# Four output-weight loads of a segment wait for the fourth step of their product instead of the first

## The chip, the cores and the metric

The program runs on one core of a Trainium2 chip. Inside a core TensorE (PE in the profile) multiplies, with its weight loads shown as PEld; VectorE (DVE), ScalarE (ACT) and GpSimd (POOL) work on rows; SyncE (SP) only issues transfers. Sixteen DMA engines carry every transfer between HBM and the on-chip memory, whoever issues it. The metric is the device time of one execution in microseconds, as a median over runs.

## The reference

Four layers run one after the other on 2048 rows of 640 values, in the order A, B, A, B, each added to its own input. Layer A is attention with a memory that is carried from segment to segment; it is the layer that the change is in.

```python
mem = mem0                                   # 8 rows of 640
for s in range(n_seg):                       # 64 segments of 32 rows
    h = concat([mem, x[32*s:32*s+32]])       # 40 rows
    q, k, v = h @ Wq, h @ Wk, h @ Wv         # 32 heads of 192: three weights of 640 x 6144
    p = softmax(mask(q k^T * 192**-0.5))     # per head, 40 x 40
    o = (p v, all heads side by side) @ Wo   # 6144 x 640
    mem = o[:8]                              # enters the next segment
    outs.append(o[8:])
```

So the 64 segments of a layer A can't run side by side: the eight memory rows of one segment are the input of the next. Layer B is a linear attention without such a chain, and the change doesn't touch it.

## The kernel before

**Layers and stages.** Each layer A has a preparation (`A_pre`), which multiplies the last eight rows of every segment for all segments at once, and the chain (`A_chain`), which runs the 64 segments in turn. In the profile the two chains lie at about 210 to 1345 us and 1840 to 2985 us.

**One segment.** The 32 heads are worked in four rounds of eight heads, numbered by their place n = 0 to 3 in the segment. Even segments take the rounds in the order 0, 1, 2, 3 and odd ones in the order 3, 2, 1, 0, so that the last round's weights of one segment are the first round's of the next. For each place n PE makes three products, Q, K and V (`project`, the matmuls of L1092). A product has five steps, i = 0 to 4, one for each block of 128 of the 640 inputs, and a step is four matmuls on four strips of the array. Between them come the scores (`scores`, L1129), the weighting of the values (`attend`, L1142, and `attend_tails`, L1155) and the output product (`wo_round`, L1198), which adds each round's part to the bank `ps_w`. The order of all instructions is the one written (a manual schedule), engine by engine.

**Which weights stay and which are loaded.** Most of the weights lie on the chip for the whole chain. Rounds 0 and 3 share places: three blocks of Q, two of K and two of V (`SLOTS`), of 384 KB each, and blocks 4 to 11 of the output weight, which lie in `wo_both` and are loaded in four pieces of 320 KB. Every segment therefore loads seven blocks through `load_slot` (L725) and four pieces through `load_piece` (L774) from HBM, all issued by SP, in one order: Q, Q, Q, K, K, V, V and then the four pieces. The pieces come in the order that `load_both` gives, columns 1280, 2560, 3840 and then 0. Here they are called pieces 1 to 4.

**What releases a load.** A load may overwrite its place only when the first round has used it. Beyond that, each load waits for one chosen matmul, so that few are under way at once: the load is put on the list `held`, and `release` takes the first of the list and makes SP wait for the matmul it is given. The table `PACE` says, for a product (m, n), after which of its five steps the next held load is released:

```python
if PACE.get((m, n)) == i:
    self.release(last)          # last: the fourth matmul of step i
```

The seven blocks are released during Q0 to Q2 (that is, Q at place 0 to Q at place 2). `load_both` puts the four pieces on the list after the output product of the first round's blocks 4 to 11, which is the last reader of `wo_both`; they are then released one by one in the products K2, V2, Q3 and K3. In the last segment of each chain all its twelve remaining loads are released together by that output product, and the table does nothing to them.

**Who uses the pieces.** The output product of the last round comes at the end of the segment, as 24 matmuls of L1198 that read `QK`. It takes blocks 6 to 11 first (pieces 1 to 3), then blocks 0 to 5, so that piece 4 (blocks 4 and 5) is used by the last four matmuls. Blocks 0 to 3 are on the chip.

**Other transfers of a segment.** POOL issues small ones on a queue of its own: `Vp<-vb` (L1073), which brings the prepared value rows of the memory's tail, `kqb<-kqb` (L1062), the rows of the next segment and the stores of the results. PE's own instructions also arrive by DMA, as packets of the instruction queue.

Of the kernel before, what the change touches and what calls it, by code (L numbers as in the profile page):

```python
# [25 lines left out]

VH = 194

PACE = {("Q", 0): 0, ("K", 0): 1, ("V", 0): 3, ("Q", 1): 4, ("K", 1): 4, ("V", 1): 3, ("Q", 2): 1, ("K", 2): 0, ("V", 2): 0,
        ("Q", 3): 0, ("K", 3): 0}  # L30

STEPS = (2, 5)

# [92 lines left out]
class Kernel:  # L126
# [876 lines left out]
    def A_chain(self, xn_dram, at_dram, li, load_slot, piece, late_wo, load_both, wo, low):  # L1003
# [3 lines left out]
        with tc.tile_pool(name=f"A{li}_ch", reuse_waits="tile", bufs=1) as sp, \  # L1007
# [67 lines left out]
            def project(hT, ps, m, n, s, steps):  # L1075
# [3 lines left out]
                for i in steps:  # L1079
# [14 lines left out]
                    if n == 0 and b >= KC - ns:  # L1094
                        self.held.append(lambda b=b: load_slot(m, order[NR - 1], b))
                    if PACE.get((m, n)) == i:
                        self.release(last)
# [371 lines left out]
```

## Time and profile before

| | us |
|---|---|
| time, median of 3 runs | 3256.92 (3249.77 to 3258.15) |
| profiled execution, first to last instruction (its span; the profile gives no other time for it) | 3253.7 |
| PE busy in it | 3095.3 (95%) |
| PEld busy | 1980.2 (61%) |
| DVE busy | 2208.8 (68%) |
| ACT busy | 1883.0 (58%) |
| POOL busy | 1410.7 (43%) |
| mean load on the 16 DMA engines in the first chain (200 to 1340 us) | share 0.74, 247 GB/s |

The page of the profile gives busy times, the span in slices, the DMA queues, the chain of work that ended last and the costliest groups. Of a group the columns are line, engine, operation, out<-in, count, busy time, mean of one in ns, and the idle time of the engine before it with what ended most of it. In the timeline each row has its start and length in us, and in square brackets the idle time of the engine before it with what ended it; "issue" there means that nothing which the profile shows ended it. The view of one line or tile gives, for transfers, the least, median and greatest time from issue to landing.

### The profile page before, as it was taken

The page shows a single profiled execution, that of the slowest core. Times are in us where ns is not written, and L with a number is a line of the kernel's source. Part 1 is how long each engine was busy: PE and PEld are TensorE (multiplying, and loading weights), DVE is VectorE, ACT ScalarE, POOL GpSimd, SP SyncE. Part 2 cuts the span into 40 slices and gives each one's busy share as a digit, 9 for nine tenths or more (in the row PEclk, how much of TensorE's full clock was granted, in tenths as well). Part 3 has the DMA queues.
Part 4 walks back from the last instruction along what each step waited for, and adds up shares of the span by engine and source line. Part 5 has one row for each costly group of instructions (what it writes and reads, how often), then busy time and mean ns, then how long its engine had stood idle before and what let it go on. Part 6 is the DMA issues. An engine that isn't in the chain of part 4 may idle for free.

```text
span 3253.7 us, 140890 instructions
## 1 busy us (share of the span) xinstructions
PE 3095.3 (95%) x59424; PEld 1980.2 (61%) x59730; DVE 2208.8 (68%) x5457; ACT 1883.0 (58%) x4481; POOL 1410.7 (43%) x2920
## 2 busy tenths in 40 slices
PE   9989999999999999999999899999999999999999
PEld 7756666666666666555367566666666666665553
DVE  5557777777777777666643577777777777776465
ACT  3346666666666666646433466666666666666453
POOL 3345555555455455430122355555555554554300
PEclk9999999999999999999999999999999999999999
DMA  8977777777777777840385677777777777778400
GB/s 306 372 271 253 256 248 257 232 255 253 236 256 245 244 257 238 285 166 1 113 319 193 240 233 257 248 252 256 242 264 240 259 244 245 255 236 282 149 1 33
DMA packets 325018, 747.58 MB, mean 230 GB/s; under 512 B 65818, under 2 KB 100274, under 8 KB 321314
## 3 DMA queue, kind: packets, MB, share of 16 engines
q1 hardware_dynamic: 254850, 638.55, 56.1%
q0 software_dynamic: 67616, 86.77, 9.7%
q10 hardware_dynamic: 1920, 13.24, 1.0%
q8 instruction: 469, 7.68, 1.0%
q14 instruction: 163, 1.34, 0.1%
HBM read 668.80 MB, written 77.03 MB: 229 GB/s over the span
## 4 chain that ended last, share of the span: by engine, by line
PE 75%; DMA 11%; DVE 8%; issue 3%; ACT 3%; POOL 0%; SPq 0%; PEld 0%; DVEq 0%; POOLq 0%; ACTq 0%
PE ps_qk_q L1092 12%; PE ps_qk_k L1092 12%; PE ps_v L1092 11%; PE ps_w L1198 10%; DMA arena<-in_A_Wv_dram 6%; PE ps_pre L960 6%; PE ps_s L1129 5%; PE ps_o L1142 3%; PE ps_pre L989 3%; PE kv L1424 2%; DVE raws L1371 2%; PE ps_wo L444 2%; DMA Vp<-vb 2%; DMA arena<-wo_rows 2%; DVE hT L1373 2%
## 5 line engine op out<-in xcount | busy, mean ns | idle before, releaser
L1092 PEld LDWEIGHTS <-hT 128*32 128x32 bf16 x30720 | 792.6, 97 | 422.7 <-issue 43.0
L1112 DVE STREAM_TRANSPOSE QK<-raws 128x512 bf16<-128x512 bf16 (+1 forms) x1152 | 730.7, 643 | 207.3 <-ACT raws L1107 166.7
L1092 PE MATMUL ps_qk_q<-arena,hT 128*32 128x384 bf16 x10240 | 510.4, 327 | 38.2 <-DVE hT L1373 31.1
L1069 POOL COPY QK<-kqb 64x192 bf16<-64x192 bf16 x1024 | 350.4, 342 | 380.9 <-PE ps_s L1129 344.3
L1092 PE MATMUL ps_qk_k<-arena,hT 128*32 128x384 bf16 x10240 | 511.7, 328 | 3.1 <-issue 1.2
L1107 ACT ACTIVATE raws<-ps_qk_k 128x512 bf16<-128x512 f32 (+1 forms) x640 | 313.5, 510 | 253.1 <-PE ps_qk_k L1092 253.1
L1092 PE MATMUL ps_v<-arena,hT 128*32 128x384 bf16 x8192 | 435.2, 326 | 15.2 <-DMA arena<-in_A_Wv_dram 7.2
L1073 POOL DMA_DIRECT2D Vp<-vb x512 | 257.6, 503 | 416.3 <-PE ps_t L1155 252.0
L1172 ACT ACTIVATE raws<-ps_o,rc 128x192 bf16<-128x192 f32 x1024 | 373.4, 420 | 109.3 <-DVE rc L1166 104.8
L1107 ACT ACTIVATE raws<-ps_qk_q 128x512 bf16<-128x512 f32 x512 | 305.7, 597 | 164.5 <-PE ps_qk_q L1092 153.4
L1198 PE MATMUL ps_w<-arena,under 128*32 128x320 bf16 x6144 | 307.4, 300 | 16.7 <-issue 13.1
L1062 POOL DMA_DIRECT2D kqb<-kqb x512 | 290.6, 568 | 70.2 <-POOL QK L1069 50.2
L1121 DVE CAST Vp<-ps_v 64x384 bf16<-64x384 f32 x512 | 286.4, 559 | 37.9 <-ACT Vp L1119 22.8
L1129 PEld LDWEIGHTS <-QK 128*80 128x80 bf16 x4096 | 195.8, 121 | 161.4 <-issue 157.3
L1119 ACT ACTIVATE Vp<-ps_v 64x384 bf16<-64x384 f32 x512 | 246.4, 481 | 55.5 <-PE ps_v L1092 54.2
L1129 PE MATMUL ps_s<-QK 128*80 128x80 bf16 x4096 | 256.8, 210 | 5.4 <-POOL QK L1069 2.8
L1218 ACT ACTIVATE E<-ps_s 80x320 bf16<-80x320 f32 x512 | 217.6, 425 | 32.3 <-PE ps_t L1155 28.9
L1051 ACT ACTIVATE wh<-ps_w 64x160 f32<-64x160 f32 x256 | 76.6, 299 | 264.8 <-DVE raws L1371 254.9
L1058 POOL DMA_DIRECT2D attn<-under x128 | 91.6, 716 | 292.8 <-DVE under L1054 289.7
L960 PEld LDWEIGHTS <-arena 128*128 128x128 bf16 x1920 | 188.4, 98 | 32.4 <-DVE next_xT L97 4.6
L97 DVE CAST arena<-ps_pre 128x512 bf16<-128x512 f32 (+1 forms) x160 | 102.2, 646 | 143.5 <-PE ps_pre L960 96.4
L1142 PE MATMUL ps_o<-Vp,E 80*32 80x193 bf16 x4096 | 180.3, 248 | 13.2 <-DMA Vp<-vb 3.7
(159 smaller groups left out, 4586.2 us busy)
## 6 DMA issues: line engine op xcount, KB each, us to landing
arena<-wo_rows SPq DMA_DIRECT2D x560, 320.0 KB, 5.6
arena<-in_A_Wq_dram SPq DMA_DIRECT2D x427, 384.0 KB, 4.3
arena<-in_A_Wk_dram SPq DMA_DIRECT2D x298, 384.0 KB, 4.8
arena<-in_A_Wv_dram SPq DMA_DIRECT2D x290, 384.0 KB, 6.0
kqb<-kqb POOLq DMA_DIRECT2D x512, 48.0 KB, 4.9
vb<-arena POOLq DMA_DIRECT2D x128, 97.0 KB, 6.1
Vp<-vb POOLq DMA_DIRECT2D x512, 24.2 KB, 4.0
kqb<-arena SPq DMA_DIRECT2D x8, 1536.0 KB, 10.0
```

Source lines behind the costliest of these rows:

```text
L960: nc.tensor.matmul(ps[:, T * i:T * i + T], lhsT=w[b][:, P * c:P * c + P], rhs=xBT[:, b, :], start=(b == 0), stop=(b == KC - 1))
L1062: nc.gpsimd.dma_start(out=kqb[:], in_=self.kqb_d[r, :, s, :])
L1069: nc.gpsimd.tensor_copy(out=o, in_=kqb[h, :].rearrange("p (x c q) -> p x c q", c=3, q=16))
L1073: nc.gpsimd.dma_start(out=Vs[n % 2][64:80, :], in_=self.vb_d[s, r].rearrange("g t f -> (g t) f"))
L1092: last = nc.tensor.matmul(o, lhsT=hT[:, b, :], rhs=rhs, start=(i == 0), stop=(i == KC - 1), tile_position=(0, 32 * g), skip_group_check=True)
L1107: nc.scalar.activation(out=raw[:, c], in_=ps[:, c], func=ACT.Copy)
L1112: nc.vector.transpose(out=o, in_=i)
L1121: nc.vector.tensor_copy(out=o, in_=i)
L1129: nc.tensor.matmul(S[0:80, c0:c0 + 80], lhsT=KT[:, 4 * x + c, :], rhs=QT[:, 4 * x + c, :], start=(c % 2 == 0), stop=(c % 2 == 1), skip_gro ...
L1142: nc.tensor.matmul(O[G][32 * h:32 * h + 32, VH * G:VH * G + 193], lhsT=E[0:80, 80 * h + 32 * G:80 * h + 32 * G + 32], rhs=V[0:80, VH * h:V ...
L1172: nc.scalar.activation(out=out, in_=i, func=ACT.Copy, scale=rc[G])
L1198: step = nc.tensor.matmul(W[q:q + 32, 0:320], lhsT=OT[i // 6][:, i % 6 // 2, 32 * (i % 2):32 * (i % 2) + 32], rhs=rhs, start=(first and i ...
```

## The change

Four numbers of the table change: the four pieces of the output weight are released by step i = 3 of the products K2, V2, Q3 and K3, not by step i = 0. The same loads, in the same order on SP, wait for a matmul that stands twelve matmuls later in the same product. No instruction is added, removed or moved on any engine.

```diff
 PACE = {("Q", 0): 0, ("K", 0): 1, ("V", 0): 3, ("Q", 1): 4, ("K", 1): 4, ("V", 1): 3,
-        ("Q", 2): 1, ("K", 2): 0, ("V", 2): 0,
-        ("Q", 3): 0, ("K", 3): 0}
+        ("Q", 2): 1, ("K", 2): 3, ("V", 2): 3,
+        ("Q", 3): 3, ("K", 3): 3}
```

More of the change, by code (lines that the diff above doesn't have):

```diff
@@ L27 @@
 VH = 194
-PACE = {("Q", 0): 0, ("K", 0): 1, ("V", 0): 3, ("Q", 1): 4, ("K", 1): 4, ("V", 1): 3, ("Q", 2): 1, ("K", 2): 0, ("V", 2): 0,
-        ("Q", 3): 0, ("K", 3): 0}
+PACE = {("Q", 0): 0, ("K", 0): 1, ("V", 0): 3, ("Q", 1): 4, ("K", 1): 4, ("V", 1): 3, ("Q", 2): 1, ("K", 2): 3, ("V", 2): 3,
+        ("Q", 3): 3, ("K", 3): 3}
 STEPS = (2, 5)
```

## The prediction

> **What bounds the kernel now.** First the page: who is busy, and what the chain that ended last is made of.
>
> ```profile
> span 3253.7 us, 140890 instructions
> PE 3095.3 (95%) x59424; PEld 1980.2 (61%) x59730; DVE 2208.8 (68%) x5457; ACT 1883.0 (58%) x4481; POOL 1410.7 (43%) x2920
> ...
> q8 instruction: 469, 7.68, 1.0%
> ...
> PE 75%; DMA 11%; DVE 8%; issue 3%; ACT 3%; POOL 0%; SPq 0%; PEld 0%; DVEq 0%; POOLq 0%; ACTq 0%
> ```
>
> PE carries the span; the rest that can be had is 11% DMA and 3% "issue". So the second view is PE's list of waits (total us, times, longest us).
>
> ```profile
> PE ps_w L1198 <- issue: 25.1, 40, 1.6
> PE ps_w L1198 <- DMA arena<-wo_rows: 9.4, 17, 1.2
> ...
> PE ps_v L1092 <- DMA arena<-in_A_Wv_dram: 7.2, 18, 0.9
> PE ps_v L1092 <- issue: 7.0, 12, 1.2
> ...
> PE ps_o L1142 <- DMA Vp<-vb: 3.7, 10, 1.0
> ...
> PE ps_o L1142 <- issue: 3.0, 3, 1.1
> ```
>
> The waits that a weight load can touch are few: 7.2 us for V blocks, 9.4 us for output weights (some of them in the chains' last segments, which the table doesn't reach), 3.7 us for the small `Vp` loads, and 35.1 us in the rows that end in "issue" (25.1 + 7.0 + 3.0). That is 55.4 us, 1.7% of the span, over 126 segments.
>
> Third, one segment without a stall, from SP's and PE's timelines. SP issues three Q, two K, two V and then the four pieces; the next segment's first Q follows at 909.42.
>
> ```profile
> 891.48 2.56 SPq L725 DMA_DIRECT2D arena<-in_A_Wq_dram  x3
> ...
> 899.05 3.55 SPq L774 DMA_DIRECT2D arena<-wo_rows  x4
> 909.42 0.33 SPq L725 DMA_DIRECT2D arena<-in_A_Wq_dram  x1
> ...
> 898.67 0.98 PE L1092 MATMUL ps_qk_k<-arena,hT 128*32 128x384 bf16 x20
> 899.49 0.34 PE L1142 MATMUL ps_o<-Vp,E 80*32 80x193 bf16 x8
> ...
> 906.94 1.00 PE L1198 MATMUL ps_w<-arena,QK 128*32 128x320 bf16 x24
> 907.77 1.03 PE L1205 MATMUL ps_idle<-arena,ident 128*32 128x512 bf16 x4
> ```
>
> **The delay.** A product starts 0.82 us before what follows it (899.49 - 898.67), so one of its five steps is 0.164 us, and three steps are 0.49 us. Each of the four issues moves by that, if nothing else holds it; 4 pieces x 126 segments = 504 transfers. Nothing is added on any engine, and the order on SP is the same. Behind piece 4 on SP stands only the next segment's first Q block, 7.1 us later (909.42 against 902.3), which waits for its own matmul. POOL, ACT and DVE are passed by nothing. So the issue side costs nothing; its cover is those 7 us.
>
> **Does a later issue land later?** The lines below are, in turn, the two kinds of load in the first chain (weight blocks, then pieces), piece 4 of the segment above, and piece 4 of two segments in which a wait of PE happened to delay SP, each with SP's row for the segment's first load.
>
> ```profile
> DMA to landing us min/median/max: 2.9/4.6/8.3
> ...
> DMA to landing us min/median/max: 4.4/5.5/7.7
> ...
> L774 SPq DMA_DIRECT2D arena<-wo_rows x1: 319/319/319, 902.3 to 902.3; - x1
> DMA to landing us min/median/max: 4.6/4.6/4.6
> ...
> 2445.33 2.44 SPq L725 DMA_DIRECT2D arena<-in_A_Wq_dram  x3
> L774 SPq DMA_DIRECT2D arena<-wo_rows x1: 320/320/320, 2456.5 to 2456.5; - x1
> DMA to landing us min/median/max: 4.2/4.2/4.2
> ...
> 2150.53 2.44 SPq L725 DMA_DIRECT2D arena<-in_A_Wq_dram  x3
> L774 SPq DMA_DIRECT2D arena<-wo_rows x1: 320/320/320, 2162.0 to 2162.0; - x1
> DMA to landing us min/median/max: 4.2/4.2/4.2
> ```
>
> A load can land 2.9 us after issue, but the pieces never take less than 4.4 in that chain: they queue behind the weight blocks. Counted from the segment's first load, piece 4 was issued after 10.8, 11.2 and 11.5 us in the three segments (902.3 - 891.48, and so on) and landed after 15.4, 15.4 and 15.7. Delays of 0.4 and 0.7 us moved the landing by 0.0 and 0.3. The load on the DMA engines in the first of them agrees:
>
> ```profile
> 903.00:905.00 2.00, 2.00 (x56) 1.32 (x48) 1.70 (x6) 1.80 (x6) 1.08 (x2) 1.00 1.04 392
> 905.00:907.00 2.00, 1.90 (x60) 1.23 (x52) 1.43 (x6) 1.05 (x3) 1.77 (x5) 1.00 0.50 160
> ```
>
> The last two columns are the share of the 16 engines and GB/s; the third from the end is the granted clock, full. The engines are full until about 905, 2.2 us after piece 4 would be issued in the new order (902.8). So I take the landing of a piece as set by the queue ahead of it, and the price of the delay itself as zero. Its bounds: nothing from below, and from above all of it on the path in every segment, 126 x 0.49 = 62 us. I take zero because the two late rows are the very experiment, but the slack is thin: piece 4 is used by the last four of the 24 final matmuls, at 906.94 + 20/24 x 0.83 = 907.63, and landed at 906.9.
>
> **What gets ahead of the pieces.** If the queue is first come, first served on each DMA engine, whatever is requested inside the four windows of 0.49 us now passes one piece. Two things can. The `Vp` load of the last round, here in one segment in the crowded and in the quiet part:
>
> ```profile
> L1073 POOL DMA_DIRECT2D Vp<-vb x1: 501/501/501, 564.6 to 564.6; - x1
> DMA to landing us min/median/max: 5.2/5.2/5.2
> ...
> L1073 POOL DMA_DIRECT2D Vp<-vb x1: 497/497/497, 570.7 to 570.7; - x1
> DMA to landing us min/median/max: 2.1/2.1/2.1
> ```
>
> 24 KB take 3.1 us longer when the weights are on their way, so POOL's loads do queue with them. It is issued close to piece 2 in every segment. A piece of 320 KB at the 392 GB/s above is 0.8 us of queue; passing it would remove most of a wait of 3.7 us in all. I take half, 1.8 us, for the two issues may land in either order.
>
> PE's own code is the second. The "issue" waits fall inside runs of equal matmuls, with weight loads stopped as well, shortly after a packet of the instruction queue:
>
> ```profile
> q8 instruction: 1, 0.02, 3.7%
> ...
> 571.77 0.53 PEld L1198 LDWEIGHTS <-raws 128*32 128x32 bf16 x19 [1.33 <-issue]
> ...
> L725 SPq DMA_DIRECT2D arena<-in_A_Wv_dram x122: 327/328/1577, 211.3 to 1324.3; - x122
> ```
>
> The first row is the window 569 to 570.7: one packet, 3.7% of 16 x 1.7 us, so 1.0 us long. I read these waits as code that arrives late because it queues too. The last row gives the segment: 61 segments from 211.3 to 1324.3, 60 steps of 18.55 us. Four windows are 1.96 us, 10.6% of it; 10.6% of 35.1 us is 3.7 us gained (if requests are spread evenly, which no row shows).
>
> Against it: code that passes piece 4 makes that piece up to 1.0 us later. 469 packets over 3253.7 us are 2.7 in a segment, 337 in 126; 0.49/18.55 of them, 8.9, fall in that window. The slack above is 0.7 us, so such a piece costs 0.3 us: 2.7 us lost. Pieces 1 to 3 have the time of the pieces behind them to spare and cost nothing; were that gone, the case is the first rival.
>
> V blocks are issued before all pieces and keep their 7.2 us; the 9.4 us for output weights stay. Sum: -1.8 - 3.7 + 2.7 = -2.8 us, from 3253.7 to 3250.9. The median of the runs is 3.2 us above this span (3256.92), so 3254.1; I say 3254. What is late next, where a `Vp` or code wait goes, is piece 4, which is why I don't take more.
>
> One rule speaks against the two gains. The Trainium skill (DMA: Bandwidth & Descriptors, "Queues, rings and completion order") says that each DMA engine takes turns between its queues, a packet at a time, so a small load on another queue shouldn't wait for a long line of weights. By that rule nothing would be passed. The two `Vp` rows, 5.2 against 2.1 us, don't look like it, but they don't exclude it.
>
> **The rivals.**
>
> Nothing moves at all: code and `Vp` wait no less than before, since they don't stand in one line with the pieces, and the pieces land when they did. The time is that of before, 3257. For it: the zero price above; against it: 5.2 against 2.1 us. Inside 0.3% (9.8 us, about what runs of this kernel can tell) it can't be told from the forecast.
>
> Slower: piece 4 lands later with its issue. Place: the last four matmuls of the final output product. In a segment without other waits piece 4 is needed 5.3 us after its present issue (907.63 - 902.3). With the whole 0.49 passed on, a segment pays as soon as the present landing takes over 4.85 us. The median landing of the pieces is 5.5, so at least half of the segments pay; where other waits already push the need back they pay less, and I take 0.3 us: 126 x 0.5 x 0.3 = 19 us, 3276. It decides from a passed-on delay of about 0.25 us. For it: the thin slack, and that piece 4 has the least queue ahead of it, since the engines drain from 905 on. Against it: the two late rows.
>
> Faster: the code requests that end in waits are not spread evenly but lie in the very windows, since the long "issue" waits are at the end of the segment. If half of the 35.1 us goes, with all 3.7 of `Vp`: -21 us, 3236. V blocks, with less traffic beside them, could add at most 7.2. For it: waits of 1.0 us and over in `ps_w`, behind the pieces in time. Against it: piece 4 then holds many of these segments.
>
> That the change doesn't do what it says would need SP to reach the pieces after their releases; its rows show it idle before each of them.
>
> **How the numbers follow.** Forecast (small net gain) 0.32 and nothing moves 0.12, together 0.44 within 0.3%; slower 0.30; faster 0.26. I put slower above faster because a late piece is paid in every segment, and a gain only in the few that wait. The range goes to the centres of the outer two and a little beyond, 3234 to 3281, which leaves out less than half of each; the forecast's own range is 3247 to 3261.
>
> **What would show it.** Right: SP's rows for the four pieces start 0.49 us later after the segment's first load, the pieces' median landing falls from 5.5 to about 5.0, the `Vp` wait halves, the `wo_rows` wait stays at some 9 us. Wrong on the slow side: landing still 5.5, `ps_w` waiting for `wo_rows` by tens of us. Wrong on the fast side: the "issue" waits of `ps_w` down by half. The forecast also fails if the V blocks' 7.2 us change, for it gives them no part.

## The result and the profile after

The changed kernel takes 3234.53 us (median of 6 runs, 3227.41 to 3239.41); the kernel before took 3255.47 us beside it (median of 6, 3244.99 to 3258.15). The ratio is 0.9932, 95% interval 0.9914 to 0.9949: 21 us faster, where a gain of 3 us was forecast. The range of 3234 to 3281 held it only at its lower edge.

The page of the changed kernel, the same rows as before:

```profile
span 3231.8 us, 140890 instructions
PE 3098.2 (96%) x59424; PEld 1978.1 (61%) x59730; DVE 2208.4 (68%) x5457; ACT 1885.5 (58%) x4481; POOL 1410.4 (44%) x2920
...
q8 instruction: 469, 7.68, 1.0%
...
PE 80%; DMA 8%; DVE 7%; ACT 3%; issue 2%; POOL 0%; SPq 0%; PEld 0%; DVEq 0%; POOLq 0%; ACTq 0%
```

The work is the same to the instruction. 21.9 us of span are gone, and in the chain that ended last DMA went from 11% to 8% and "issue" from 3% to 2%. PE's list of waits (total us, times, longest) says which:

```profile
PE ps_w L1198 <- issue: 13.4, 25, 1.5
PE ps_w L1198 <- DMA arena<-wo_rows: 11.1, 26, 1.2
...
PE ps_v L1092 <- issue: 7.9, 14, 1.1
...
PE ps_v L1092 <- DMA arena<-in_A_Wv_dram: 6.6, 12, 1.9
...
PE ps_o L1142 <- DMA Vp<-vb: 1.4, 4, 0.5
...
PE ps_o L1142 <- issue: 0.2, 1, 0.2
```

The wait of `ps_w` that ends in "issue" fell from 25.1 to 13.4 us and that of `ps_o` from 3.0 to 0.2, the wait for `Vp` from 3.7 to 1.4. The wait for V blocks hardly moved (7.2 to 6.6), and that for the output weights rose by 1.7 us (9.4 to 11.1).

All rows of PE's wait list together fell by 24.8 us (139.4 to 114.6), and PE's busy time rose by 2.9. The rows that the prediction counts (three of "issue", `Vp`, V blocks, output weights) make 14.8 us of it; of the rest the largest is the wait for Q blocks, 5.7 to 3.4 us.

One segment shows the change and what came of it: the segment at 555.47 us of the profile before, whose 1.33 us stop of the weight loads the prediction quotes. First SP in that segment, its first load and its pieces before the change, then all its rows in the changed kernel:

```profile
555.86 2.44 SPq L725 DMA_DIRECT2D arena<-in_A_Wq_dram  x3
...
563.43 3.55 SPq L774 DMA_DIRECT2D arena<-wo_rows  x4
```

```profile
549.95 2.44 SPq L725 DMA_DIRECT2D arena<-in_A_Wq_dram  x3
553.04 1.68 SPq L725 DMA_DIRECT2D arena<-in_A_Wk_dram  x2
555.30 0.81 SPq L725 DMA_DIRECT2D arena<-in_A_Wv_dram  x2
558.01 3.55 SPq L774 DMA_DIRECT2D arena<-wo_rows  x4
567.88 0.33 SPq L725 DMA_DIRECT2D arena<-in_A_Wq_dram  x1
```

The pieces start 8.06 us after the segment's first load (558.01 - 549.95), against 7.57 us (563.43 - 555.86) before: 0.49 us later. Then PE's last output products in that segment, before the change and after it:

```profile
570.34 0.43 PE L1198 MATMUL ps_w<-arena,raws 128*32 128x320 bf16 x5
571.77 0.73 PE L1198 MATMUL ps_w<-arena,raws 128*32 128x320 bf16 x16 [1.00 <-issue]
```

```profile
564.33 1.00 PE L1198 MATMUL ps_w<-arena,raws 128*32 128x320 bf16 x24
565.41 1.00 PE L1198 MATMUL ps_w<-arena,QK 128*32 128x320 bf16 x24
```

Before, PE ran 5 of 24 matmuls and stopped for 1.00 us; after, the 24 run through. The place is no accident. This is segment 20 of the first chain, counted from 0, and before the change segments 4, 36 and 52 stop after the same fifth matmul (rows of the timeline before):

```profile
278.04 0.86 PE L1198 MATMUL ps_w<-arena,raws 128*32 128x320 bf16 x19 [0.87 <-issue]
...
869.97 0.86 PE L1198 MATMUL ps_w<-arena,raws 128*32 128x320 bf16 x19 [0.92 <-issue]
...
1167.60 0.86 PE L1198 MATMUL ps_w<-arena,raws 128*32 128x320 bf16 x19 [0.86 <-issue]
```

Of these four stops two are gone after the change, one shrank to 0.22 us and one stayed at 1.04. A stop that comes back at the same point of the program every sixteen segments, with weight loads and matmuls both idle, fits code that arrives in packets of a fixed size (7.68 MB in 469 packets, 16 KB each). No row names it, but the times of the packets in the trace do. In the kernel before, all 30 "issue" waits of over 0.5 us on PE's lines L1092, L1129, L1142 and L1198 end 1.2 to 1.6 us after the end of an instruction packet; only 7% of all moments in a chain lie there.

The packets can also be compared by their number, for all kernels have 469. Times are counted from the segment's first product, and `quarter_pieces`, a kernel of the experiments whose pieces have a quarter of the bytes, is the measure. The 200 packets that start there 10.5 to 16.5 us into a segment start 1.05 us later in the kernel before (mean), and 0.65 us later in the changed kernel. The 90 packets of the first 6 us, ahead of all pieces, differ by less than 0.1 us. So the code that is late is the code that comes while pieces are in the queue, and the change brings it forward by 0.4 us.

Time from issue to landing, least, median and greatest in the first chain: the pieces in the changed kernel, and the `Vp` load of the segment above (issued at 558.7, 5.2 us before the change).

```profile
DMA to landing us min/median/max: 4.0/4.9/7.0
...
DMA to landing us min/median/max: 4.4/4.4/4.4
```

The pieces' median fell from 5.5 to 4.9 us, by the delay of 0.49 us and a little more: they land when they did. The `Vp` load lands 0.8 us sooner, the time of one piece. Over all segments the trace says the same: the `Vp` load beside piece 2 is issued 0.10 us after it before the change and 0.38 us ahead of it afterwards, and its median to landing falls from 5.15 to 4.43 us (124 segments each).

### The profile page after: what moved, and what is told of

It is laid out like the page before. It is cut to its first block, busy times and chain, and to the rows that moved or that the text cites. A ratio compares the mean times of both kernels' runs of the same rounds, so it can differ in the third digit from the quotient of the medians.

```text
span 3231.8 us, 140890 instructions
## 1 busy us (share of the span) xinstructions
PE 3098.2 (96%) x59424; PEld 1978.1 (61%) x59730; DVE 2208.4 (68%) x5457; ACT 1885.5 (58%) x4481; POOL 1410.4 (44%) x2920
## 3 DMA queue, kind: packets, MB, share of 16 engines
q8 instruction: 469, 7.68, 1.0%
## 4 chain that ended last, share of the span: by engine, by line
PE 80%; DMA 8%; DVE 7%; ACT 3%; issue 2%; POOL 0%; SPq 0%; PEld 0%; DVEq 0%; POOLq 0%; ACTq 0%
PE ps_qk_q L1092 13%; PE ps_qk_k L1092 13%; PE ps_v L1092 12%; PE ps_w L1198 10%; PE ps_pre L960 7%; PE ps_s L1129 6%; DMA arena<-wo_rows 4%; DMA arena<-in_A_Wv_dram 3%; PE ps_pre L989 3%; PE ps_o L1142 3%; PE kv L1424 2%; DVE raws L1371 2%; PE ps_wo L444 2%; DVE hT L1373 2%; PE ps_pq L495 1%
## 5 line engine op out<-in xcount | busy, mean ns | idle before, releaser
L1092 PEld LDWEIGHTS <-hT 128*32 128x32 bf16 x30720 | 788.5, 96 | 418.2 <-issue 38.1
L1092 PE MATMUL ps_qk_q<-arena,hT 128*32 128x384 bf16 x10240 | 509.1, 327 | 34.8 <-DVE hT L1373 29.8
L1092 PE MATMUL ps_qk_k<-arena,hT 128*32 128x384 bf16 x10240 | 509.5, 327 | 3.3 <-ACT raws L1107 1.0
L1092 PE MATMUL ps_v<-arena,hT 128*32 128x384 bf16 x8192 | 434.9, 326 | 15.0 <-issue 7.9
L1198 PE MATMUL ps_w<-arena,under 128*32 128x320 bf16 x6144 | 304.5, 300 | 7.2 <-issue 3.8
L1129 PEld LDWEIGHTS <-QK 128*80 128x80 bf16 x4096 | 195.1, 120 | 161.5 <-issue 157.4
L1129 PE MATMUL ps_s<-QK 128*80 128x80 bf16 x4096 | 255.7, 210 | 3.1 <-POOL QK L1069 2.9
L99 ACT ACTIVATE arena<-ps_pre 128x512 bf16<-128x512 f32 (+1 forms) x160 | 92.9, 595 | 163.0 <-PE ps_pre L960 107.4
```

The source lines that it names most:

```text
L1092: last = nc.tensor.matmul(o, lhsT=hT[:, b, :], rhs=rhs, start=(i == 0), stop=(i == KC - 1), tile_position=(0, 32 * g), skip_group_check=True)
L1129: nc.tensor.matmul(S[0:80, c0:c0 + 80], lhsT=KT[:, 4 * x + c, :], rhs=QT[:, 4 * x + c, :], start=(c % 2 == 0), stop=(c % 2 == 1), skip_gro ...
L1198: step = nc.tensor.matmul(W[q:q + 32, 0:320], lhsT=OT[i // 6][:, i % 6 // 2, 32 * (i % 2):32 * (i % 2) + 32], rhs=rhs, start=(first and i ...
```

## The experiments

All were timed against the kernel before on their own chip, so ratios are compared, not times. Three theories stood at the start, named in the expectations: order (what is asked for in the windows passes a piece), room (V blocks gain), and chance (where the code packets happen to fall).

### Two pieces at a time, three, and a step further

`first_two_late`, `last_two_late`, `first_three_late` and `fifth_step` set the four numbers to these (here and below the end of the table is written in one line):

```diff
-        ("Q", 2): 1, ("K", 2): 0, ("V", 2): 0, ("Q", 3): 0, ("K", 3): 0}
+        ("Q", 2): 1, ("K", 2): 3, ("V", 2): 3, ("Q", 3): 0, ("K", 3): 0}   # first_two_late
+        ("Q", 2): 1, ("K", 2): 0, ("V", 2): 0, ("Q", 3): 3, ("K", 3): 3}   # last_two_late
+        ("Q", 2): 1, ("K", 2): 3, ("V", 2): 3, ("Q", 3): 3, ("K", 3): 0}   # first_three_late
+        ("Q", 2): 1, ("K", 2): 4, ("V", 2): 4, ("Q", 3): 4, ("K", 3): 4}   # fifth_step
```

> Only pieces 1 and 2 are released by the fourth step (K2 and V2: 3); pieces 3 and 4 stay at the first. Theory 1 (order: code packets and Vp loads that are asked for in the 0.49 us windows pass one piece; landings stay): two of the four windows, and the Vp load is issued next to piece 2, so a good half of the 21 us, 3241 to 3247 us; median Vp landing of the last round falls as in the changed kernel. Theory 2 (room: V blocks land sooner because pieces 1 and 2 leave the engines to them): nearly all of it, 3234 to 3238 us, with the waits for V blocks down. Theory 3 (chance: only how the code packets fall against the segments): anything between 3230 and 3258 us.

> Only pieces 3 and 4 are released by the fourth step (Q3 and K3: 3). Theory 1: a little under half, 3244 to 3250 us, waits that end in issue down by some 5 us, Vp landing as before the change. Theory 2: nothing, 3253 to 3258 us, because the V blocks have left the engines before piece 3. Theory 3: anything between 3230 and 3258 us.

> Pieces 1 to 3 by the fourth step, piece 4 by the first, as before. Theory 1: piece 4 is the only one with little slack, so the loss by it is spared and a fourth of the windows is given up: 3232 to 3242 us, and the wait of ps_w for wo_rows not above that before the change. Theory 2: as the changed kernel, 3232 to 3237 us. Theory 3: anything between 3230 and 3258 us.

> All four pieces by the fifth step (4), so 0.65 us after the first. Theory 1: windows a third longer, but piece 4 lands later in more segments: 3228 to 3238 us. Theory 2: the V blocks have a little more room, 3230 to 3236 us. Theory 3: anything between 3230 and 3258 us.

Measured: 0.9940 (0.9919 to 0.9961), 0.9957 (0.9938 to 0.9977), 0.9909 (0.9888 to 0.9930) and 0.9917 (0.9896 to 0.9937). The last two pieces alone bring 0.43%, where room gave them nothing: room is out as the only cause. The three first pieces bring all there is; the fifth step no more than the fourth. One expectation failed: with piece 4 left where it was, the wait for the output weights should not rise, and in `first_three_late` it is 13.3 us for 9.4.

### One piece at a time

Two and two left open which piece lets what pass, so each was moved alone, from 0 to 3: K2 (`only_piece1`), V2 (`only_piece2`), Q3 (`only_piece3`), K3 (`only_piece4`).

```diff
-        ("Q", 2): 1, ("K", 2): 0, ("V", 2): 0, ("Q", 3): 0, ("K", 3): 0}
+        ("Q", 2): 1, ("K", 2): 0, ("V", 2): 0, ("Q", 3): 3, ("K", 3): 0}   # only_piece3; the others alike
```

> Only piece 1 by the fourth step (K2: 3). Order theory: code asked for in that one window passes it; the Vp load is issued 0.7 us later and passes nothing. 0.0 to 0.3% faster, Vp waits as before (3 us or more), issue waits 30 to 38 us. Room theory: this piece stands directly behind the V blocks, so if those gain by room, it is here: V waits under 4 us and 0.3% or more.

> Only piece 2 by the fourth step (V2: 3). Order theory: the Vp load, issued 0.1 us after piece 2 before and 0.4 us ahead of it now, passes it in every segment: Vp waits under 1.5 us, Vp median to landing down by 0.1 us or more over all, 0.1 to 0.4% faster. Room theory: nothing beyond 0.1%.

> Only piece 3 by the fourth step (Q3: 3). Order theory: the code whose late arrival stops ps_w is asked for around here, so the issue waits of ps_w fall from 25 us to 20 or less, 0.1 to 0.4% faster, Vp waits as before. Room theory: nothing.

> Only piece 4 by the fourth step (K3: 3). Order theory: some code passes piece 4, but what passes it makes it late: issue waits of ps_w at or under 22 us, the wait of ps_w for wo_rows 9 to 14 us, 0.0 to 0.2% faster. Room theory: nothing, or slower by 0.1%.

Measured: 0.9977 (0.9964 to 0.9991), 0.9964 (0.9947 to 0.9982), 0.9956 (0.9940 to 0.9972) and 0.9997 (0.9987 to 1.0008). Each carries something else. PE's waits with piece 2 alone, then with piece 3 alone:

```profile
PE ps_w L1198 <- issue: 22.2, 34, 1.7
...
PE ps_o L1142 <- DMA Vp<-vb: 1.2, 2, 0.9
```

```profile
PE ps_w L1198 <- issue: 10.8, 21, 1.5
PE ps_o L1142 <- DMA Vp<-vb: 8.8, 15, 1.3
```

Piece 2 frees the `Vp` load, which POOL issues beside it, and leaves the code waits of `ps_w` nearly as they were. Piece 3 more than halves those code waits and does nothing for `Vp`. That profile is of the fastest run of `only_piece3` (3241.27 us; its median is 3254.02), but both readings hold over all profiles with pieces of full size (all but the two of the quarter pieces below). With piece 3 released later the code waits of `ps_w` are 4.4 to 17.7 us (ten profiles), without it 19.5 to 25.1 (six); with piece 2 later the wait for `Vp` is 0.0 to 1.9 us (ten), without it 3.7 to 9.7 (six). Piece 4 brings nothing on the whole, though the expectation allowed it up to 0.2%. Piece 1 brings 0.23% that its profile doesn't place: of the four sums in the table below only that for V blocks is lower than before the change (5.1 us), and its span, 3259.4 us, was above that of before. The four add up to 1.06% against the 0.68% of all together. Perhaps what one piece frees is partly taken back by the next thing that is late; the intervals, about 0.1 to 0.2% to either side of each of the five, are too wide to show it.

### A whole product later

```diff
-        ("Q", 2): 1, ("K", 2): 0, ("V", 2): 0, ("Q", 3): 0, ("K", 3): 0}
+        ("Q", 2): 1, ("V", 2): 0, ("Q", 3): 0, ("K", 3): 0, ("V", 3): 0}
```

> Each piece is released by the first step of the next product (V2, Q3, K3, V3), which delays them by 1.07, 0.81, 1.35 and 1.27 us (the distances of those products in the segment at 898.67 us of the profile before). Theory 1: twice the windows, so up to twice the gain from order, but piece 4, issued 1.27 us later, now lands after its 907.63 us point in most segments; its loss of some 0.3 to 0.8 us in 126 segments outweighs the rest: 3240 to 3290 us, with ps_w waiting for wo_rows by 20 us or more. Theory 2: V blocks at their best, the same late piece 4: 3240 to 3290 us. The waits that end in issue tell the two apart: under theory 1 they fall below those of the changed kernel, under theory 2 they stay.

Measured: 0.9994 (0.9978 to 1.0010), no gain and no loss. PE's waits show both sides of it:

```profile
PE ps_w L1198 <- DMA arena<-wo_rows: 38.9, 67, 1.5
PE ps_v L1092 <- issue: 9.1, 14, 1.6
PE ps_w L1198 <- issue: 4.4, 12, 0.7
```

The code waits of `ps_w` go on falling, to 4.4 us, and the wait for the output weights goes from 9.4 to 38.9 us. By the trace 31.6 of these 38.9 us stand before the 21st of the 24 final matmuls, the first that uses piece 4; there it is 0.8 us in the kernel before and 4.0 in the changed one. This is the forecast's slow rival, met at a delay of 1.27 us for piece 4 and not at 0.49.

### Small pieces

`quarter_pieces` is the kernel before with a quarter of each piece loaded, `quarter_pieces_late` the changed kernel with the same edit. Both leave out the other three quarters, so the last round multiplies with old weights there and the result is not that of the reference; the matmuls are the same in number.

```diff
-            ... out=into[:, c:c + 1280], in_=self.wo_rows[r, :, own + c:own + c + 1280])
+            ... out=into[:, c:c + 320], in_=self.wo_rows[r, :, own + c:own + c + 320])
```

> The releases of before, but each piece loads 320 of its 1280 columns, 80 KB for 320; the last round then multiplies with old weights, so this part of the output product is left out of the computation. The queue loses 0.96 MB of 4 MB in a segment, all behind the V blocks. Theory 1: code and Vp loads no longer queue behind pieces, so issue waits in the chains fall from 36.8 us to under 15 and Vp waits from 3.6 to under 1; V waits stay near 7.0: 3215 to 3235 us. If the issue waits have nothing to do with the pieces they stay at 30 us or more, and the time at 3245 to 3256 us.

> The same quarter pieces (80 KB, the rest of the last round's output weights left out), released by the fourth step as in the changed kernel. Theory 1: with 0.2 us of queue to a piece there is nothing left to pass, so within 5 us of the quarter pieces released by the first step. Theory 2: the V blocks still profit, some 5 us or more faster than those. Theory 3: anything within 15 us of it.

Measured: 0.9815 (0.9794 to 0.9837) and 0.9822 (0.9800 to 0.9843). PE's waits in the first:

```profile
PE ps_w L1198 <- DMA arena<-wo_rows: 6.1, 12, 0.8
PE ps_v L1092 <- issue: 6.1, 14, 1.3
...
PE ps_v L1092 <- DMA arena<-in_A_Wv_dram: 3.8, 9, 0.7
...
PE ps_w L1198 <- issue: 3.4, 5, 1.2
```

With a quarter of the bytes the code waits of `ps_w` are 3.4 us for 25.1, and the later release brings nothing more. So the pieces' bytes make that code late, and with little left to pass there is nothing to gain from the order. The time fell further than I expected (3202 us, not 3215 to 3235).

### Chance

`before_code_shifted` and `after_code_shifted` move PE's code against the segments, with the releases of before and of the changed kernel.

```diff
-FILL = {0: 65, 2: 79}
+FILL = {0: 73, 2: 87}
```

> The kernel before, with eight more one-column weight loads in the first segment of each chain (FILL 73 and 87 for 65 and 79). Eight instructions move every later packet of PE's code against the segments by half of the 16-instruction grid in which packets fall over 16 segments. If the gain is chance (where the packets happen to fall), this kernel moves by itself by 5 to 20 us to either side. If the packets sample the segment closely enough, it stays within 6 us of the kernel before: 3252 to 3264 us, with issue waits of 30 to 42 us in the chains.

> The changed kernel with the same eight weight loads. If order in the queue is the cause: still 0.5 to 0.9% under the kernel before, issue waits of 18 to 27 us in the chains. If chance: the difference from the kernel with the same shift and the old releases is no longer near 21 us.

Measured: 0.9992 (0.9975 to 1.0010) and 0.9922 (0.9900 to 0.9944). The kernel before stays where it was and the changed one keeps its gain; at this one shift, then, the gain doesn't hang on where the packets fall. The profile of the first was its slowest run (3275.5 us of span), and shows how much one execution differs from another:

```profile
PE ps_w L1198 <- issue: 24.8, 34, 1.6
...
PE ps_o L1142 <- DMA Vp<-vb: 9.2, 19, 0.9
```

The code waits of `ps_w` repeat (25.1, 24.8), those for `Vp` don't (3.7, 9.2).

### Where Vp stands, and combinations

`vp_behind` is the changed kernel with two of POOL's issues exchanged; `three_late_vp_behind` is `first_three_late` with the same exchange; `three_fifth_step` has 4, 4, 4, 0.

```diff
-                    if n != 2:
-                        tails_after(n)
                     fetch_kq(s, n)
+                    if n != 2:
+                        tails_after(n)
```

> The changed kernel, with POOL issuing the kqb load before the Vp load, so that Vp comes 0.6 us later and stands behind piece 2 again, as before the change. Theory 1 with Vp as a large part: Vp waits come back to 3 us or more and the time rises by 4 to 10 us above the changed kernel, 3238 to 3246 us. If code alone carries the gain: 3232 to 3237 us.

> Pieces 1 to 3 by the fourth step, piece 4 by the first, and the kqb load issued before the Vp load. The two best versions together; both gains are of the same kind and the Vp wait is already small, so no sum of the two: 3225 to 3236 us. Over 3236 us would say that a later Vp load costs where piece 4 isn't late.

> Pieces 1 to 3 by the fifth step, piece 4 by the first. Pieces 1 to 3 have slack for it and piece 4 keeps its place: 3228 to 3238 us, issue waits at or under the 22 us that three pieces at the fourth step left, ps_w waiting for wo_rows under 6 us. If the last 0.16 us bring nothing: 3232 to 3238 us.

Measured: 0.9919 (0.9894 to 0.9943), 0.9934 (0.9911 to 0.9956) and 0.9929 (0.9905 to 0.9953). The exchange did not do what the expectations assume. The `Vp` load waits for PE (`ps_t`) in any case, and in the trace its issue still stands 0.39 us ahead of piece 2 in `vp_behind` and `three_late_vp_behind`, against 0.38 in the changed kernel: only the `kqb` load moved. So the wait of 1.4 us for `Vp` in `vp_behind` and the times of both kernels say nothing of a later `Vp` load; `only_piece2` does. In `three_fifth_step` the wait for the output weights is 13.5 us where under 6 was expected, again with piece 4 left in its place. None of the five variants near the changed kernel differs from it by more than the intervals, so none is shown to be better.

### All waits side by side

The sums below add the rows of PE's wait list: all that end in "issue" on the chain's lines (`ps_w`, `ps_v`, `ps_o`, `ps_s`, `ps_t`, `ps_qk`, and `ps_idle` where it has one), and the three that end in a load.

| kernel | code ("issue") | Vp | V blocks | output weights | sum | span of that run |
|---|---|---|---|---|---|---|
| before | 37.5 | 3.7 | 7.2 | 9.4 | 57.8 | 3253.7 |
| changed | 22.3 | 1.4 | 6.6 | 11.1 | 41.4 | 3231.8 |
| only_piece1 | 43.1 | 9.7 | 5.1 | 10.5 | 68.4 | 3259.4 |
| only_piece2 | 35.2 | 1.2 | 6.1 | 13.5 | 56.0 | 3247.1 |
| only_piece3 | 22.4 | 8.8 | 5.4 | 7.9 | 44.5 | 3239.6 |
| only_piece4 | 35.2 | 8.7 | 11.5 | 10.4 | 65.8 | 3262.8 |
| next_product | 18.0 | 0.2 | 1.9 | 38.9 | 59.0 | 3254.8 |
| quarter_pieces | 11.7 | 0.3 | 3.8 | 6.1 | 21.9 | 3198.0 |
| before_code_shifted | 46.8 | 9.2 | 9.4 | 11.1 | 76.5 | 3275.5 |
| after_code_shifted | 27.7 | 0.0 | 4.9 | 11.9 | 44.5 | 3238.5 |

A straight line through the 18 profiles (kernel before, changed kernel and all sixteen experiments) gives 1.3 us of span for 1 us of listed wait, with a correlation of 0.97; without the two kernels with quarter pieces it is 1.1 us and 0.98. So most of what sets these executions apart lies in these four waits.

## Why the prediction was wrong

**The delay** was right: 0.49 us, nothing queued behind it on SP.

**The landing of the pieces** was right. Zero price at 0.49 us: the median went from 5.5 to 4.9 us, where about 5.0 was forecast, and the wait for output weights rose by 1.7 us.

**What gets ahead of the pieces** was right as a mechanism. This part named both things that pass, the `Vp` load and PE's code, and why; `only_piece2` and `only_piece3` show them one by one, and the times of the `Vp` loads and of the code packets show both come sooner.

**The code term is the step that failed.** It said: "10.6% of 35.1 us is 3.7 us gained (if requests are spread evenly, which no row shows)". The same three rows went from 35.1 to 21.5 us (13.4 + 7.9 + 0.2), so 13.6 us; in the two kernels with shifted code they differ by 12.4 us (38.9 and 26.5). The windows are 10.6% of a segment, but the code that PE later waits for isn't drawn evenly from it: it is the code that comes while pieces are in the queue. The packets behind the 30 long waits of the kernel before all start 10.3 to 15.4 us into their segment, within less than a third of its 18.55 us. `only_piece3` halves the code waits of `ps_w` with one window of 2.6%, and `quarter_pieces` shows that nearly all of those in `ps_w` come from the pieces (3.4 us are left). The share should have been taken of the requests that end in a wait, not of all time. The long waits stood in `ps_w`, late in the segment, and the forecast names that under its fast rival, but counts with the even share.

**The Vp term** was too small, by a row from one execution. It took half of 3.7 us, 1.8; the row fell by 2.3. The reason for the half, that the two issues may land in either order, was not in the trace: the `Vp` load was issued 0.10 to 0.12 us after piece 2 in all 124 segments. In the other profiles with pieces of full size in which piece 2 is released by the first step as before, the same wait is 5.4 to 9.7 us (`last_two_late` 5.4, `only_piece4` 8.7, `before_code_shifted` 9.2, `only_piece1` 9.7), and with piece 2 moved it is 0.0 to 1.9.

**The loss at piece 4**, 2.7 us, had the right sign and size, but its cause stays open. Before the 21st of the final matmuls the wait went from 0.8 to 4.0 us; the whole row for output weights rose by 1.7, and differs by as much between the kernel before and its shifted copy (9.4 and 11.1). At that matmul it is 4.1 us with piece 2 alone moved, 4.9 with pieces 1 to 3 and 2.8 with piece 4 alone, so code that passes piece 4 is not the whole of it.

**V blocks** were given no part; 7.2 became 6.6. Right for the whole change; that piece 1 alone gains 0.23% stays unexplained.

**The rivals.** "Nothing moves at all" fell: order in the queue is worth 0.7%. With it fell what I drew from the rule of turns in the Trainium skill (DMA: Bandwidth & Descriptors, "Queues, rings and completion order"), that nothing would be passed; the `Vp` load went from 5.15 to 4.43 us, and how an engine chooses between its queues isn't shown by these runs. "Slower" needs a longer delay: at 1.27 us for piece 4 it takes all the gain. "Faster" came out by its own mechanism, but that 21 us were forecast and 21 measured is partly luck: its terms are 17.5 us of code and 3.7 of `Vp`, their rows fell by 13.6 and 2.3, and the rest of the gain stands in rows that it doesn't name. It had 0.26, below "slower", on the argument that a late piece is paid in every segment and a gain only in the few that wait. But the two late rows had already taken the price from the first half of that argument, and the waits listed, 55.4 us, were larger than the 19 us of the slow rival.

## What to carry to other kernels

Where transfers queue on engines that are full, it is worth trying to issue a load with slack later, within its slack. Here at 0.49 us it lands when it did, and small transfers that PE needs sooner, its own code among them, go ahead of it; at 0.65 us nothing more came of it, and at 0.81 to 1.35 us the gain was lost. Gaps of PE in the middle of a run of equal matmuls, with weight loads idle too and nothing named as the cause, belong in the sum of what the transfers cost. The end of an instruction packet at a fixed distance before each such gap tells whether it is code. When a delay frees such waits, look at which requests end in a wait before taking a share of the time.

## What the runs showed of the hardware

A packet of PE's code, 16 KB and about 1.0 us long, can be kept back behind ordinary weight loads: in the second half of a segment it started 1.05 us later on average than with a quarter of the output weights' bytes. In the kernel before, stops of PE that end 1.2 to 1.6 us after such a packet took up to 1.6 us each; all "issue" waits, the short ones included, came to 37.5 us, and with a quarter of the bytes to 11.7. A delay of 0.49 us in the issue of 320 KB loads left their landing where it was (median from issue 5.5 to 4.9 us), and moved a 24 KB load on another queue forward by 0.7 us (median 5.15 to 4.43).
